# Sliding-window attention and a highway layer in one kernel: the first pair of batches by query blocks, the highway layer on two blocks at a time, the last x transposed by DMA

## The chip, the cores and the metric

The kernel runs on one core of a Trainium2 chip. That core has five engines with instruction queues of their own: PE (TensorE: matrix products and transposes, with results in PSUM), DVE (VectorE), ACT (ScalarE), POOL (GpSimd) and SP (SyncE, which here issues stores). Each engine runs its queue in order and waits on semaphores of the others. The metric is the device time of one execution in microseconds (us).

## The reference

Eight batches, eight heads, 576 positions, head dimension 64. Attention looks back over 128 positions, with a linear bias per head; its output x (4608 rows of 512) goes through a highway layer.

```python
scores = scale * np.matmul(q, k.transpose(0, 1, 3, 2))
rel = pos[:, None] - pos[None, :]
bias = slopes[:, None, None] * (-np.abs(rel))[None, :, :]
mask = (rel >= 0) & (rel < 128)
scores = np.where(mask, scores + bias[None], -1e9)
attn = softmax(scores)                       # max, exp, sum, divide
x = np.matmul(attn, v).transpose(0, 2, 1, 3).reshape(B * S, H * D)
H_ = np.maximum(x @ w_h, 0.0)
T_ = 1.0 / (1.0 + np.exp(-(x @ w_t + b_t)))
out = T_ * H_ + (1.0 - T_) * x
```

Inputs and output are float32; inside the kernel most tiles are bf16, and POOL's loads convert on the way.

## The kernel before, in words

**Duos and stages.** Batches are handled in four duos (m = 0 to 3) of two batches (r = 0, 1). A sequence of 576 positions is four blocks of 128 and a tail block of 64. Duos 1 to 3 have two attention stages each, A (key blocks 0 and 1) and B (key blocks 2, 3 and the tail, 4); duo 0 has four smaller ones, a to d, one for each key block (d also has the tail).

**Loads.** POOL issues the loads that convert. Q and K of a duo come with four neighbouring positions in one partition (L113: 1 KB runs in memory, 512 bytes in SBUF), V and the tails with one position in a partition (L125, L118: 256 bytes in memory, 128 in SBUF). For duo 0, Q and K are cut in two halves of 256 positions, the first half also in two groups of heads. The weight wT comes through POOL (L234), the bias row through L232. The weight wH comes through SP as float32 into the buffer that later takes Q of duo 1 (L222) and is converted by ACT (L228).

**Attention.** PE transposes Q and K (L271; tails L257); DVE or ACT copies the result from PSUM to the tiles `qt` and `kt` (L290, L296, L283). For each head, score products of 64 rows (L329) go to PSUM, the two batches on the two halves of the rows; ACT takes the exponential with the key part of the bias (L345) into `pt`; DVE multiplies by a mask with the rest (L364); PE multiplies with V, which has a column of ones (L393); DVE takes the reciprocal of the sums and writes x (L409, L410).

**Highway layer, block by block (36 blocks of 128 rows).** PE transposes x in four steps (L433), ACT copies it to `xt` (L442), PE makes the product with wH in four matmuls of 512 columns (L449), DVE makes u = max(h, 0) - x (L456), PE makes the product with wT in four (L465) and adds the bias row by a fifth matmul with a one-hot left operand (L467), ACT takes tanh of half of it (L473), POOL (for the last blocks DVE) makes t = 0.5 tanh + 0.5 (L478), DVE multiplies u by t (L483), POOL adds x into the float32 tile `ot` (L489; the very last block DVE), and SP stores it in four parts (L505; the tail blocks in two, L497).

**What sets the order.** All steps are nodes in a dictionary, each with an engine, a planned cost, a priority and dependencies. The order in which they are issued is not computed in the kernel: a list of 762 numbers, `ISSUE`, gives it, and a list `BANKS` gives the PSUM bank (of eight) that each step takes. Since every engine runs in order, these lists set each engine's queue. The SBUF tiles come from small pools: three buffers each of x, `uu`, `tt` and `ot`, five of `xt`. The planned costs serve the search for the order only; they are in the code (`node(..., cost, ...)`), among them 1250 ns on SP and 1000 ns to land for a block of x transposed by DMA, a step (`f_xd`) that the kernel before has and does not use, its list `DMA_X` being empty.

In PE's queue the steps of attention of one duo lie between highway steps of the duo before. After the last product of weights and V there are seven highway blocks left.

Of the kernel before, what the change touches and what calls it, by code (L numbers as in the profile page):

```python
# [14 lines left out]
def kernel(  # L15
# [30 lines left out]
        "a": ((0, 0, 0), (0, 1, 128)),  # L46
        "b": ((1, 1, 0), (1, 2, 128)),
        "c": ((2, 2, 0), (2, 3, 128)),
        "d": ((3, 3, 0), (3, 4, 128), (4, 4, 192)),
    }  # L50
    ORDER = ("abcd", "AB", "AB", "AB")
    DMA_X = ()

    HOME = {"A": ("A", 0), "B": ("B", 0), "a": ("A", 0), "b": ("A", 256), "c": ("B", 0), "d": ("B", 256)}

    GROUPS = {
        "A": ((0,), (1,), (2,), (3,)), "B": ((0,), (1,), (2,), (3,), (4,)),
        "a": ((0,), (1,)), "b": ((0,), (1,)), "c": ((0,), (1,)), "d": ((0,), (1,), (2,)),
    }

    ADD_MASK = ()
# [36 lines left out]
    def load_qk(m, w, x=None, hs=None):  # L98
        src, dst = ((q, QL), (k, KL))[w]
        ps = slice(0, P) if x is None else slice(64 * x, 64 * x + 64)  # L100
        for r in (slice(0, 2),) if hs is None else (0, 1):
            hh = slice(0, H) if hs is None else slice(4 * hs, 4 * hs + 4)
            if hs is None:
                o = dst[m % 2][ps].rearrange("p r h n -> p (r h) n")
                i = src[2 * m : 2 * m + 2, :, 4 * ps.start : 4 * ps.stop, :].rearrange(
                    "r h (p t) d -> p (r h) (t d)", t=4
                )
            else:
                o = dst[m % 2][ps, r, hh, :]
                i = src[2 * m + r, hh, 4 * ps.start : 4 * ps.stop, :].rearrange(  # L110
                    "h (p t) d -> p h (t d)", t=4
                )
            nc.gpsimd.dma_start(out=o, in_=i)  # L113
# [22 lines left out]
    MKA = ADD_MASK and cp.tile([P, H, 2 * P], BF16, name="mka")  # L136
    cvec = cp.tile([P, H], F32, name="cvec")
    ones1 = cp.tile([P, P], BF16, name="ones1")
    wH = cp.tile([P, NCK, DM], BF16, name="wH")
# [25 lines left out]


    BIG = float(2**20)

    def c_mka():
        nc.vector.tensor_scalar(out=MKA[:, :, 0:P], in0=bc(tri[:, 0, :], P), scalar1=BIG,  # L170
                                scalar2=-BIG, op0=ALU.mult, op1=ALU.add)
        for h in range(H):
            nc.vector.tensor_scalar(
                out=MKA[:, h, P : 2 * P], in0=tri[:, 1, :], scalar1=BIG,
                scalar2=-BIG - P * slopes[h] / scale, op0=ALU.mult, op1=ALU.add,
            )

# [13 lines left out]
    def c_vec():  # L191
        nc.vector.memset(ones1[:], 0.0)
        nc.vector.memset(ones1[0:1, :], 1.0)
        nc.vector.memset(bT[:], 0.0)
        for h in range(H):
            nc.vector.memset(cvec[:, h : h + 1], float(np.exp(-float(P) * slopes[h])))
# [20 lines left out]

    def w_stage():
        return QL[1][:].rearrange("p r h n -> p (r h n)").bitcast(F32)

    def load_wf():
        nc.sync.dma_start(  # L222
            out=w_stage().rearrange("p (c n) -> p c n", c=NCK),
            in_=moe_w_h.rearrange("(c p) n -> p c n", p=P),
        )

    def cast_wf():
        nc.scalar.copy(out=wH[:].rearrange("p c n -> p (c n)"), in_=w_stage())  # L228

    def load_w(n):  # L230
        if n == 2:
            nc.gpsimd.dma_start(out=bT[0:1, :], in_=moe_b_t.rearrange("(o n) -> o n", o=1))  # L232
# [10 lines left out]
    def chunks(m):  # L243
        return (0, 1) if ORDER[m][0] == "a" else (None,)

    def tr_parts(m):

        ps = [(x, hs) for x in chunks(m) for hs in range(4 if x is None else 2)]
        return ps + ["tail"]

    def transposes(m, w, part):
# [11 lines left out]
        x, hs = part  # L263
        L = (QL, KL)[w][i]
# [12 lines left out]
    def evac(m, w, part):  # L277
# [7 lines left out]
        x, hs = part  # L285
        nh, n0, n = (2, 0, P) if x is None else (4, 64 * x, 64)
# [14 lines left out]
    def width(kind):  # L301
        return 512 if kind in "AB" else 256

    def scores(m, kind, h):
        i, W = m % 2, width(kind)
        if W == 512 or h % 2 == 0:
            SC[m, kind, h] = ps_tile(2)
        else:
            SC[m, kind, h] = SC[m, kind, h - 1]
        sc, o = SC[m, kind, h], 0 if W == 512 else (h % 2) * W  # L310
        qm = QT[i][:, h, 0:512].rearrange("p (t c q) -> p c t q", t=4, c=4)
        segs, n, add = STAGES[kind], 0, m == 0 and kind in ADD_MASK
        if add and h % 2 == 0:
            for r in range(2):
                nc.tensor.matmul(
                    out=sc[:, r, :], lhsT=ident[:],
                    rhs=MKA[:, h : h + 2, :].rearrange("p h n -> p (h n)"),
                    start=True, stop=False,
                )
        while n < len(segs):  # L320
            j, qb, off = segs[n]
            two = n + 1 < len(segs) and segs[n + 1][0] == j and segs[n + 1][1] < 4
            for r in range(2):
# [3 lines left out]
                else:  # L327
# [4 lines left out]
                    rhs=rhs, start=not add,  # L332
                    stop=not add or (h % 2 == 1 and n + 1 + two >= len(segs)),
# [3 lines left out]
    def soft(m, kind, h):  # L337
        W, (home, c0) = width(kind), HOME[kind]
        if h % 2 == 0:
            if c0 == 0:  # L340
                PT[m, home, h // 2] = ptp[home].tile([P, 2, 2, 512], BF16, name="pt")
            for j, qb, off in STAGES[kind]:
                COL[m, h // 2, j, qb] = (PT[m, home, h // 2], c0 + off)
        o = 0 if W == 512 else (h % 2) * W
# [447 lines left out]
```

The softmax here doesn't subtract the row's maximum and nothing guards it: scores larger than these inputs give would overflow.

## Time and profile before

| what | value |
|---|---|
| time, median of 11 runs | 174.98 us (174.52 to 176.22) |
| profiled execution: its own time | 176.02 us |
| profiled execution: span of the instructions | 174.3 us |
| PE busy | 149.2 us (86%), 2109 matmuls |
| DVE / ACT / POOL busy | 139.9 / 125.2 / 118.6 us |
| loads by POOL's queue | 14.68 MB as written to SBUF, 62832 packets |
| transfers by SP's queue (stores, wH) | 10.49 MB, 7312 packets |

The profile is of one execution. Spans count from its first instruction. A busy time is the time in which an engine ran an instruction; a row of a group gives line, engine, operation, output and inputs, count, and then busy time, the mean of one in ns, and the idle time before them with what ended it. The chain of waits is the work that ended last, followed back through what released each step; the lines of it give start, length and what ran. In the stretches, the columns are: from and to, length, then the busy time of PE, of PE's weight loads, of DVE, ACT and POOL, each with the number of instructions, then the clock granted to PE, the share of the DMA engines and GB/s moved.

### The profile page before, as it was taken

To read this page: it belongs to the slowest core of one execution; us is meant where nothing else is said; L and a number is where in the kernel's file an instruction comes from. 1 tells how busy PE (TensorE), PEld (TensorE's weight loads), DVE (VectorE), ACT (ScalarE), POOL (GpSimd) and SP (SyncE) were. 2 spreads that over 40 slices of the span, in tenths; PEclk is the share of its full clock that TensorE was granted. 3 is DMA by queue.
4 is the path that set the end of the run, shared out by engine and by line. 5 is a ranking of instruction groups with operands and counts; after the bars stand their busy time and mean duration, and the time that the engine had idled before them with its cause. 6 is when DMAs were issued, how large, how long until landed. Compare 5 with 4: busy or idle time off the path is not lost.

```text
span 174.3 us, 5232 instructions
## 1 busy us (share of the span) xinstructions
PE 149.2 (86%) x2109; PEld 92.9 (53%) x2132; DVE 139.9 (80%) x244; ACT 125.2 (72%) x178; POOL 118.6 (68%) x132
## 2 busy tenths in 40 slices
PE   0169688999989979999999979999999999999930
PEld 0158444576646537767556655566556556754410
DVE  5087596889998978999877999889887889986570
ACT  2625568597988988899679968799898887235510
POOL 7897284189893799994058886783485969676540
PEclk9999999999999999999999999999999999999996
DMA  4999999999999999999999997493224232445543
GB/s 147 225 193 190 153 197 183 180 177 114 183 197 212 194 110 152 224 216 213 250 108 163 116 183 103 76 140 101 50 66 120 64 94 72 107 113 122 129 121 90
DMA packets 70167, 25.50 MB, mean 146 GB/s; under 512 B 48128, under 2 KB 65024, under 8 KB 70144
## 3 DMA queue, kind: packets, MB, share of 16 engines
q0 software_dynamic: 62832, 14.68, 120.0%
q1 hardware_dynamic: 7312, 10.49, 22.5%
q8 instruction: 16, 0.26, 0.7%
q14 instruction: 7, 0.06, 0.1%
HBM read 30.41 MB, written 9.44 MB: 229 GB/s over the span
## 4 chain that ended last, share of the span: by engine, by line
PE 50%; DMA 19%; DVE 15%; issue 6%; POOL 4%; ACT 3%; SPq 0%; POOLq 0%; DVEq 0%; ACTq 0%
PE ps L449 13%; PE ps L465 13%; DMA va<-in_v_dram 8%; PE ps L329 7%; PE ps L393 6%; DMA ql<-in_q_dram 6%; PE ps L433 4%; DVE pt L364 4%; DMA kl<-in_k_dram 3%; PE ps L467 3%; PE ps L271 3%; DVE x L410 3%; DVE qt L290 2%; ACT pt L345 2%; DVE uu L483 2%
## 5 line engine op out<-in xcount | busy, mean ns | idle before, releaser
L345 ACT ACTIVATE pt<-ps,bias 128x1024 bf16<-128x1024 f32 (+1 forms) x80 | 72.2, 948 | 14.0 <-PE ps L329 13.8
L489 POOL TENSOR_TENSOR ot<-uu,x 128x512 f32<-128x512 bf16 x35 | 47.6, 1364 | 25.3 <-DVE uu L483 25.3
L364 DVE TENSOR_TENSOR pt<-pt,mk 128x2048 bf16<-128x2048 bf16 (+1 forms) x40 | 45.6, 1153 | 0.8 <-ACT pt L345 0.8
L449 PE MATMUL ps<-wH,xt 128*128 128x512 bf16 x129 | 35.8, 393 | 2.6 <-DVE qt L290 1.0
L465 PE MATMUL ps<-wT,xt 128*128 128x512 bf16 x136 | 36.3, 380 | 1.4 <-DVE uu L456 0.8
L473 ACT ACTIVATE tt<-ps 128x512 f16<-128x512 f32 x36 | 21.6, 604 | 13.0 <-PE ps L467 11.9
L456 DVE SCALAR_TENSOR_TENSOR uu<-ps,x 128x512 bf16<-128x512 f32 x36 | 24.5, 683 | 5.0 <-PE ps L449 4.7
L478 POOL TENSOR_SCALAR tt<-tt 128x512 f16<-128x512 f16 x32 | 22.3, 704 | 8.8 <-ACT tt L473 8.5
L329 PE MATMUL ps<-qt,kt 64*128 64x256 bf16 (+2 forms) x384 | 24.9, 249 | 3.6 <-DVE qt L290 1.1
L410 DVE TENSOR_TENSOR x<-ps,rd 128x256 bf16<-128x256 f32 (+3 forms) x40 | 25.5, 638 | 1.4
L125 POOL DMA_DIRECT2D va<-in_v_dram x20 | 22.3, 1114 | 5.8 <-DMA ql<-in_q_dram 4.1
L393 PEld LDWEIGHTS <-pt 128*128 128x128 bf16 (+1 forms) x576 | 21.0, 101 | 7.6 <-issue 2.5
L393 PE MATMUL ps<-va,pt 128*128 128x65 bf16 (+1 forms) x576 | 24.6, 198 | 0.0
L442 ACT COPY xt<-ps 128x512 bf16<-128x512 bf16 x36 | 20.7, 590 | 5.3 <-PE ps L433 4.1
L483 DVE TENSOR_TENSOR uu<-uu,tt 128x512 bf16<-128x512 bf16 x36 | 19.7, 555 | 3.6 <-POOL tt L478 3.4
L449 PEld LDWEIGHTS <-xt 128*128 128x128 bf16 x144 | 13.1, 100 | 16.0 <-issue 3.5
L329 PEld LDWEIGHTS <-kt 64*128 64x128 bf16 x384 | 13.3, 96 | 13.1 <-issue 9.1
L465 PEld LDWEIGHTS <-xt 128*128 128x128 bf16 x144 | 12.9, 97 | 13.6 <-issue 1.5
L271 PE MATMUL ps<-ident,kl 128*64 128x128 bf16 (+1 forms) x320 | 12.1, 228 | 8.2 <-DMA kl<-in_k_dram 7.9
L296 ACT COPY kt<-ps 128x1024 bf16<-128x1024 bf16 x13 | 13.1, 1016 | 5.6 <-PE ps L271 5.6
L271 PEld LDWEIGHTS <-kl 128*64 128x64 bf16 (+1 forms) x320 | 9.9, 126 | 10.0 <-DMA kl<-in_k_dram 8.5
L290 DVE COPY qt<-ps 128x1024 bf16<-128x1024 bf16 x16 | 11.0, 685 | 4.2 <-PE ps L271 4.2
(44 smaller groups left out, 125.5 us busy)
## 6 DMA issues: line engine op xcount, KB each, us to landing
out_dram<-ot SPq DMA_DIRECT2D x128, 64.0 KB, 2.7
va<-in_v_dram POOLq DMA_DIRECT2D x16, 256.0 KB, 13.6
ql<-in_q_dram POOLq DMA_DIRECT2D x3, 1024.0 KB, 15.1
kl<-in_k_dram POOLq DMA_DIRECT2D x3, 1024.0 KB, 15.2
ql<-in_moe_w_h_dram SPq DMA_DIRECT2D x1, 1024.0 KB, 5.4
out_dram<-ot SPq DMA_DIRECT2D x8, 128.0 KB, 2.4
kl<-in_k_dram POOLq DMA_DIRECT2D x4, 128.0 KB, 5.6
ql<-in_q_dram POOLq DMA_DIRECT2D x4, 128.0 KB, 5.9
```

What stands on the lines that cost most here:

```text
L125: nc.gpsimd.dma_start(out=VA[m % 2][0:n, c, :, :, 0:D].rearrange("s r h d -> s (r h) d"), in_=v[2 * m : 2 * m + 2, :, c * P : c * P + n, : ...
L271: nc.tensor.transpose(out=pt[r * D : (r + 1) * D, c : c + n], in_=L[ps, r, nh * hs + hl, t * D : (t + 1) * D], identity=ident[ps, ps],)
L329: nc.tensor.matmul(out=sc[:, r, o + off : o + off + w_], lhsT=KT[i][rows, h, j * P : (j + 1) * P], rhs=rhs, start=not add, stop=not add or ...
L345: nc.scalar.activation(out=PT[m, home, h // 2][:, h % 2, :, c0 : c0 + W], in_=SC[m, kind, h][:, :, o : o + W], func=ACTF.Exp, bias=BIAS[:, ...
L364: nc.vector.tensor_tensor(out=o, in0=o, in1=mk.to_broadcast([P, 2, rep, W]), op=ALU.mult,)
L393: nc.tensor.matmul(out=av[rows, hl, n * (D + 1) : (n + 1) * (D + 1)], lhsT=pt[:, hl, r, off : off + (D if narrow else P)], rhs=va[:, j, r, ...
L410: nc.vector.tensor_tensor(out=x.rearrange("p b (h d) -> p h b d", h=2), in0=av[:, :, :, 0:D], in1=rd[:, :, 0:nb].to_broadcast([P, 2, nb, D ...
L449: nc.tensor.matmul(out=AH[m, kind, gi], lhsT=XT[m, kind, gi][:, i, c, :], rhs=wH[:, c, :], start=c == 0, stop=c == NCK - 1)
L456: nc.vector.scalar_tensor_tensor(out=uu[:, 0:n, :], in0=AH[m, kind, gi].rearrange("p (i n) -> p i n", i=1), scalar=0.0, in1=x, op0=ALU.max ...
L465: nc.tensor.matmul(out=az, lhsT=XT[m, kind, gi][:, i, c, :], rhs=wT[:, c, :], start=c == 0, stop=False)
L483: nc.vector.tensor_tensor(out=uu, in0=uu, in1=TT.pop((m, kind, gi))[:, 0:n, :], op=ALU.mult)
L489: eng.tensor_tensor(out=ot[:, 0:n, :], in0=UU.pop((m, kind, gi))[:, 0:n, :], in1=x, op=ALU.add)
```

## The change

- **Duo 0 by query blocks.** Stages e, f, g, h have the scores that finish query block 0, 1, 2 and 3 with the tail. Q and K of blocks 0 and 1 come one position in a partition (`load_nat`, into the buffer that later takes K of duo 1), block 0 in two groups of heads; blocks 2 and 3 as before, in one piece.
- **wH through POOL.** The load through SP and the conversion on ACT are gone; wH is now loaded as wT is. In POOL's queue it is the 19th transfer, after K and Q of duo 0, its tails and V blocks 0 and 1. POOL's queue starts with K of blocks 2 and 3, then Q of block 0 (half of the heads), Q of blocks 2 and 3, and the other parts of block 0 and block 1.
- **Highway layer in pairs.** The blocks are taken two at a time (16 pairs; the four tail blocks stay single): one ACT copy, one u, one tanh, one t, one product with t for both, with two PSUM banks each for the products. The sum into `ot` stays one instruction per block. The bias of a pair is now put in first, by two matmuls of 64 rows (`f_zb`), from a second one-hot tile `hot2` and two copies of the bias row.
- **x of the last duo by DMA.** `DMA_X = (8, 9)`: for stages A and B of duo 3, `xt` is made by nine transposing DMAs on SP in place of PE transposes and ACT copies.
- **A new order.** `ISSUE` (670 numbers) and `BANKS` are new. PE's queue starts with the transposes of Q of block 0, then K and Q of blocks 2 and 3, and the scores of e follow the last transposes of block 0. After the last product of weights and V, ten highway blocks are left: the pairs of duo 3's A and B, and two tail blocks, the last steps being gate of duo 2's tail, then duo 3's tail. SP's queue has the nine transposes among the stores: both pairs of A, the second pair of B, a store, the first pair of B, three stores, the tail, and the last stores. On POOL, t and the two sums of a pair stand in a row; its last steps are t of the last pair, t of duo 2's tail, the pair's two sums and the tail's sum.
- Some planned costs are new, and unused code (an additive mask) is gone.

```diff
-        "a": ((0, 0, 0), (0, 1, 128)),
-        "b": ((1, 1, 0), (1, 2, 128)),
-        "c": ((2, 2, 0), (2, 3, 128)),
-        "d": ((3, 3, 0), (3, 4, 128), (4, 4, 192)),
+        "e": ((0, 0, 0),),
+        "f": ((1, 1, 0), (0, 1, 128)),
+        "g": ((2, 2, 0), (1, 2, 128)),
+        "h": ((2, 3, 0), (3, 3, 128), (3, 4, 256), (4, 4, 320)),
     }
-    ORDER = ("abcd", "AB", "AB", "AB")
-    DMA_X = ()
+    ORDER = ("efgh", "AB", "AB", "AB")
+    DMA_X = (8, 9)
...
-        "A": ((0,), (1,), (2,), (3,)), "B": ((0,), (1,), (2,), (3,), (4,)),
-        "a": ((0,), (1,)), "b": ((0,), (1,)), "c": ((0,), (1,)), "d": ((0,), (1,), (2,)),
+        "A": ((0, 1), (2, 3)), "B": ((0, 1), (2, 3), (4,)),
+        "e": ((0, 1),), "f": ((0, 1),), "g": ((0, 1),), "h": ((0, 1), (2,)),
...
+    def load_nat(w, b, hs):
+        src = (q, k)[w]
+        if hs is None:
+            nc.gpsimd.dma_start(
+                out=nat(w, b).rearrange("p r h d -> p (r h) d"),
+                in_=src[0:2, :, b * P : (b + 1) * P, :].rearrange("r h s d -> s (r h) d"),
+            )
+            return
+        for r in range(2):
+            hh = slice(4 * hs, 4 * hs + 4)
+            nc.gpsimd.dma_start(
+                out=nat(w, b)[:, r, hh, :],
+                in_=src[r, hh, b * P : (b + 1) * P, :].rearrange("h s d -> s h d"),
+            )
...
-    def load_wf():
-        nc.sync.dma_start(
-            out=w_stage().rearrange("p (c n) -> p c n", c=NCK),
-            in_=moe_w_h.rearrange("(c p) n -> p c n", p=P),
-        )
-
-    def cast_wf():
-        nc.scalar.copy(out=wH[:].rearrange("p c n -> p (c n)"), in_=w_stage())
...
+        if x in ("n0", "n1"):
+            hh = heads(part)
+            for h in hh:
+                for r in range(2):
+                    c = (h - hh.start) * P
+                    nc.tensor.transpose(
+                        out=pt[r * D : (r + 1) * D, c : c + P],
+                        in_=nat(w, int(x[1]))[:, r, h, :], identity=ident[:],
+                    )
+            return
...
     def f_h(m, kind, gi, i):
-        AH[m, kind, gi] = ps_tile(1)
+        n = grp(m, kind, gi)[1]
+        if i == 0:
+            AH[m, kind, gi] = ps_tile(n).rearrange("p (i n) -> p i n", i=1) if n == 1 else ps_tile(n)
         for c in range(NCK):
-            nc.tensor.matmul(out=AH[m, kind, gi], lhsT=XT[m, kind, gi][:, i, c, :],
+            nc.tensor.matmul(out=AH[m, kind, gi][:, i, :], lhsT=XT[m, kind, gi][:, i, c, :],
                              rhs=wH[:, c, :], start=c == 0, stop=c == NCK - 1)
...
+    def f_zb(m, kind, gi):
+        AZ[m, kind, gi] = ps_tile(2)
+        for i in range(2):
+            rows = slice(i * D, (i + 1) * D)
+            nc.tensor.matmul(out=AZ[m, kind, gi][:, i, :], lhsT=hot2[rows, :], rhs=bT[rows, :],
+                             start=True, stop=False)
...
-    def f_out(m, kind, gi, eng):
+    def f_out(m, kind, gi, i, eng):
         bs, n, x = grp(m, kind, gi)
-        ot = op.tile([P, 2, DM], F32, name="ot")
-        OT[m, kind, gi] = ot
-        eng.tensor_tensor(out=ot[:, 0:n, :], in0=UU.pop((m, kind, gi))[:, 0:n, :], in1=x, op=ALU.add)
+        if i == 0:
+            OT[m, kind, gi] = op.tile([P, 2, DM], F32, name="ot")
+        eng.tensor_tensor(out=OT[m, kind, gi][:, i, :], in0=UU[m, kind, gi][:, i, :],
+                          in1=x[:, i, :], op=ALU.add)
```

The step that makes `xt` by DMA is in both kernels and reads:

```python
for i in range(n):
    nc.sync.dma_start_transpose(out=xt[:, i], in_=x[:, i, :])
```

## The prediction

> **What bounds the kernel now.** I read the stretches first (busy time of each engine between two times), cut where the work changes its kind: the first highway matmul starts at 28.4 us, the last product of weights and V ends at 152.1, the last matmul at 167.1, the span at 174.3.
>
> ```profile
> 28.40:152.10 123.70, 118.06 (x1705) 74.28 (x1725) 109.62 (x178) 103.83 (x140) 86.83 (x87) 1.00 1.59 143
> 152.10:167.10 15.00, 14.77 (x81) 7.06 (x82) 10.43 (x20) 6.29 (x11) 9.85 (x11) 1.00 0.46 115
> 167.10:174.30 7.20, 0.00 (x0) 0.00 (x0) 2.14 (x4) 0.60 (x1) 1.11 (x1) 0.78 0.44 109
> ```
>
> Columns: stretch, length, busy us of PE, its weight loads, DVE, ACT and POOL, granted clock, DMA share, GB/s. From 28.4 to 167.1 us PE is busy 132.8 of 138.7 us at full clock (96%), so PE work taken out there comes off the end nearly one for one; only 5.9 us are gaps. DVE (89% of the long stretch) is the next limit. Before 28.4 and after 167.1 PE doesn't set the time.
>
> Second, the chain of waits, for what a PE step costs in the dense part:
>
> ```profile
> 106.48 0.86 PE ps L465 x4
> 107.34 0.22 PE ps L467
> ...
> 108.64 0.33 PE ps L329 x8
> ...
> 111.43 0.22 PE ps L433 x4
> ```
>
> A gate of one block is 0.86 us, its bias matmul 0.22, the four transposes of x 0.22 (0.33 elsewhere in the chain). Eight score matmuls of 256 columns take 0.33 us; at the gate's rate (0.86 us for 4 x 512 columns) they would take 0.86 one after another, so two matmuls of 64 rows, one on each half of the array, overlap.
>
> Third, the start. The chain runs through transfers until 19.5 us:
>
> ```profile
> 2.14 6.02 DMA kl<-in_k_dram
> 8.44 10.98 DMA ql<-in_q_dram
> ...
> 28.38 3.05 PE ps L449 x7
> ```
>
> ```profile
> 5.00:15.00 10.00, 5.49 (x138) 4.30 (x140) 4.65 (x7) 4.23 (x10) 9.49 (x16) 1.00 1.41 196
> 113.50:116.00 2.50, 2.50 (x48) 1.83 (x49) 1.96 (x4) 2.43 (x4) 2.30 (x2) 1.00 1.91 122
> ```
>
> Last column: 196 GB/s while Q and K come in rows of four positions (512 bytes in SBUF), 122 while only V rows (128 bytes) flow. And POOL's issues wait for old transfers:
>
> ```profile
> POOL va L125 <- DMA ql<-in_q_dram: 4.1, 1, 4.1
> POOL qtl L118 <- DMA ql<-in_q_dram: 3.1, 1, 3.1
> ```
>
> Counting issues, transfer n of POOL's queue starts only when transfer n-8 has landed; so the stream is first come, first served, and its bytes set the start.
>
> **The change, part by part** (minus is gain).
>
> 1. Bias. Removed: 36 x 0.22 = 7.9 us. Added: 4 single blocks x 0.22, and 16 pairs with two 64-row matmuls into two banks. If they overlap like the score pairs, 0.22 a pair, together 4.4, so -3.5; if not, 0.44 a pair and -0.0. I take -3.5: the score rows are the same kind of instruction. A pair's bias now stands ahead of its gates and takes two banks early: the gates queue behind a tanh that still reads them. The plan gives these banks; I charge nothing, and the cover is the 0.86-us gates of other groups.
>
> 2. x of the last duo by DMA. Removed: nine blocks x 0.22 to 0.33 on PE = 2.0 to 3.0, I take -2.4, and nine ACT copies (590 ns, 5.3 us; ACT is 84% busy, so nothing on the path). Added: nine transposing DMAs on SP, of which the trace shows none. Lower bound 0.42 us of SP each (the store's issue, L505); upper 2.7, if each went only when the one before had landed (a 64 KB store takes that long). The planner's table in the code, whose other entries agree with the rows (exp 1118 against 1118 ns), has 1.25 a block and 1 us to land; I take this. Then the last duo's first pair, asked for when its last norm ends, some 6 us before PE reaches it, takes 2.5 + 2. Hidden; +0, the upper bound is a rival. Queued behind on SP: the second pair of B waits for the duo's last norm, and three stores stand behind; their `ot` buffer is wanted again three groups later, some 8 us, against 2.5 us of transposes and 4 issues of 0.42. Covered.
> [...]
>
> 3. Pairs elsewhere. PE: two products with wH back to back save one seam (0.91 against 0.86 us in the chain): 16 x 0.05 = -0.8. ACT: 36 copies of 590 and 36 tanh of 604 ns become 12 of 1016 (L296, 128x1024) and 3 of 590, and 16 of 1118 and 4 of 604: 42.9 to 36.2 us. DVE: u 36 x 683 to 16 x 1220 (L296 on DVE) + 4 x 683, g 36 x 555 to 16 x 730 (L364, 128x1024) + 4 x 555: 44.6 to 36.2. POOL: t 704 ns each, a pair between 704 and 1408, I take 1100; `ot` sums stay one per block. All this lies beside PE: zero on the path, unless the 5.9 us of gaps shrink (a rival).
>
> 4. Start. The stream up to what the first product needs: before, wT is last: 2048 KB of Q and K at 196 GB/s (10.7), V and tails 640 KB at 122 (5.4), wT 512 KB at 196 (2.7) = 18.8 us; it landed at 26.3 (issue 14.40 + 11.9), so an offset of 7.5. After, wH comes through POOL's queue, behind 1024 KB in 512-byte rows (5.4), 1024 KB natural Q and K, 256 KB tails and 512 KB V, all in 128-byte rows (15.0), itself 2.7: 7.5 + 23.1 = 30.6. So the first product starts at about 30.8 and not 28.4: +2.4. Bounds: natural rows at the 145 GB/s seen from 18.5 to 21 us give +0.0; two of its waits for landings not covered (3.1 and 0.8 us) give +6. Against it, more is done by then. Adding the chain's step costs over the order of both kernels, the left-over PE work at that point is 125.8 us before and 118.7 after; 6.0 of the difference is counted in 1 and 2, 1.1 is new. At 1.11 (below) that is 1.2; net +1.2. The ACT cast of wH (1.9 us) goes, beside idle time.
> [...]
>
> 5. Behind the start the stream still leads: wT, tails, K of duo 1 (1024 KB, 5.4) land at 39.8, V block 2 at 41.9, Q of duo 1 at 47.3. PE, at 1.11 us per us of step costs (the dense part's own ratio: 138.7 for 125.8), reaches their users at 39.4, 42.1 and 46.0. +1.3; bounds 0 and 4. POOL's t and `ot` wait behind the blocked issues, three buffers deep: no charge.
>
> 6. Tail. Before, 15 us of PE follow the last weights-V product and 7.2 us the last matmul: 22.2. After, ten blocks (18.8 us) are left, and POOL runs t, g, two sums in a row per pair: 1.1 + 0.7 (DVE) + 2 x 1.15 = 4.1 us against 3.65 of PE. Following both by hand, POOL's last sum (block 4 of duo 2) ends 22.2 us after that product, three pairs of stores on SP (1.7 + 1.1 + 1.1) and 3.1 from last issue to end of the span follow: 28.0, which is 9.2 behind the last matmul: +2.0. Bounds: 0 (order covers POOL) and +4 (sums at 2.1 us, as some in the trace when the mask runs).
>
> Sum: -3.5 - 2.4 - 0.8 + 1.2 + 1.3 + 2.0 = -2.2 us on the profiled execution, 176.02 us long with a span of 174.3 (1.7 around it). It stands 0.6% above the median 174.98; I carry the difference over: 172.8.
>
> **Rivals.**
> A. The gaps close: DVE and ACT each lose 7 to 14 us, and the PE waits on DVE and ACT in the dense part go, 4 of 5.9 us; tail covered. For it: the waits on `qt`, `uu` and `pt` are the named ones. Against: each is 1 us or less, spread. 172.8 - 4 - 2 = 166.8.
> B, the other side. Transposing DMAs are not pipelined (2.7 us each). The last single block's x has nine of them and four stores (6.8) ahead on SP: -6 + 24.3 + 6.8 + 2 = 27 us after the last weights-V product, then 2 us of PE and 7.2 of tail: 36.3 against 28.0. 172.8 + 8.3 = 181.1. It decides from 2.0 us a block (12 + 9 x 2.0 = 30, the forecast's 28.0 and the 2.2 us gained).
> C. The stream is later still (first product at 34, duo 1's Q at 51): 3 + 2 more, 177.8. For it: small packets and POOL's waits; against: no other traffic on it.
> D. The bias pair doesn't overlap: 3.5 back, 176.3.
>
> **How the numbers follow.** About 0.3% (0.5 us) is what can be told from no change. Forecast 0.44 (own range 170 to 175.5: in it 0.35 faster, 0.05 same, 0.04 slower), A 0.23, B 0.11, C 0.16, D 0.06. Faster 0.58, same 0.05, slower 0.37. The range takes in D, C and all of A but its lower end: 166.5 to 178.5; left out are B and some 0.09 of A.
>
> **What would show it.** Right: matmuls of the bias in pairs that start together; no x transposes on PE after the last duo's scores; first wH matmul at 30 to 32 us, waiting for the wH transfer; PE over 95% busy from then to the last matmul; end 9 us behind it, last on POOL. Wrong: `xt` waits on SP's transposes, PE gaps before `kl` and `va` users beyond 50 us, or POOL far behind from the first duo on.

## The result: 1.1% slower, and the profile after

The changed kernel takes 177.1 us (median of 12 runs, 176.22 to 178.24), the kernel before 175.09 us beside it (47 runs). The ratio is 1.0109, interval 1.0084 to 1.0134. The forecast was 172.8 us, range 166.5 to 178.5: the time lies in the range, on the wrong side of no change. Ratios leave out single executions that were disturbed and ran longer, medians do not, and the profiles of the first shift, of the shift alone and of the early DMA are of such executions.

The profiled execution has an own time of 177.07 us and a span of 175.4. Its stretches, cut at the first highway matmul, at 152 us as before, at the last matmul and at the end of the span (the last product of weights and V now ends earlier, at 145.3, with ten blocks left):

```profile
28.85:152.00 123.15, 115.04 (x1669) 71.29 (x1688) 99.79 (x151) 98.56 (x106) 77.79 (x72) 0.99 1.44 146
152.00:166.79 14.79, 13.29 (x64) 5.45 (x62) 8.76 (x11) 4.25 (x5) 10.62 (x10) 1.00 0.78 193
166.79:175.40 8.61, 0.00 (x0) 0.00 (x0) 2.63 (x3) 0.60 (x1) 2.33 (x3) 0.64 0.50 122
```

The start costs 0.45 us (28.85 against 28.40), the dense part is 0.76 shorter (137.94 against 138.7), the tail 1.41 longer (8.61 against 7.2): together +1.1, the difference of the spans. The profile of before is of an execution 0.9 us above its median (176.02 against 175.09 us), that of the changed kernel is at its median; so these 1.1 us are about half of the 2.0 us between the medians, and the rest is in neither profile. The dense part is what did not deliver. In it PE is busy 128.33 us (115.04 + 13.29) where it was busy 132.8, so 4.5 us of work are gone, but its gaps have grown from 5.9 to 9.6 us. The waits of PE between 28 and 167 us name them:

```profile
PE ps L285 <- issue: 2.3, 1, 2.3
PE ps L466 <- DMA xt<-x: 1.4, 1, 1.4
PE ps L447 <- DVE x L421: 1.1, 2, 0.6
```

(Engine and line, what it waited for, total, times, longest.) The first is strange: L285 is a transpose of Q and K, and it waited for nothing that the profile shows. The chain of waits has the place:

```profile
43.44 0.64 PE ps L285 x16
44.08 0.55 PE ps L447 x8
44.63 1.89 PE ps L285 x58
46.52 2.30 issue
48.83 0.36 PE ps L285 x6
```

Groups of 32, 16 and 16 transposes run without a break. Of the last sixteen PE does ten, stops for 2.3 us, and then does the other six, which read the same tile. In all seven profiles that have the stop it lies behind the same 58 transposes. What follows, in stretches of a microsecond (the third figure from the end is the granted clock):

```profile
49.00:50.00 1.00, 1.00 (x30) 0.85 (x26) 0.69 (x1) 0.44 (x1) 0.00 (x0) 0.90 1.44 197
50.00:51.00 1.00, 0.78 (x8) 0.29 (x4) 0.66 (x2) 1.00 (x2) 0.00 (x0) 0.50 1.69 185
51.00:52.00 1.00, 1.00 (x4) 0.16 (x4) 0.63 (x2) 0.06 (x1) 0.29 (x1) 0.50 2.35 161
52.00:53.00 1.00, 1.00 (x7) 0.32 (x7) 0.00 (x0) 0.36 (x1) 1.00 (x2) 0.50 2.44 156
53.00:54.00 1.00, 1.00 (x6) 0.29 (x6) 0.08 (x1) 0.75 (x1) 1.00 (x2) 0.89 2.35 169
```

PE runs at half clock for some 3.4 us, which makes its work about 1.7 us longer (an estimate: half of 3.4; two matmuls of L466 in a row start 0.43 us apart at 51 us, and 0.22 at 53.3 us, behind it). In the profile before, the clock was 1.00 throughout the dense part. The ledger is then: PE work without the half clock 132.8 to 126.6, -6.2; half clock +1.7; gaps +3.7, which are the stop (2.3) and the wait for `xt` (1.4). Sum -0.8.

The other lines that answer to those shown of before: the chain's prices, and the start.

```profile
106.78 0.97 PE ps L466 x4
...
109.13 0.39 PE ps L483 x2
109.52 0.32 PE ps L492
```

```profile
wH<-in_moe_w_h_dram POOLq DMA_DIRECT2D x1, 512.0 KB, 8.9
```

```profile
10.00:13.00 3.00, 2.41 (x70) 2.07 (x67) 1.59 (x3) 0.30 (x4) 3.00 (x4) 1.00 2.26 153
13.00:16.00 3.00, 1.82 (x24) 1.29 (x24) 2.55 (x5) 0.66 (x2) 3.00 (x5) 1.00 2.02 129
16.00:19.00 3.00, 2.66 (x59) 2.23 (x60) 1.73 (x3) 2.59 (x7) 3.00 (x6) 1.00 2.41 153
```

The bias of a pair (L483) takes 0.39 us in the chain here, not the 0.22 that the forecast took. The natural rows of Q and K came at 129 to 153 GB/s (last column), not at 122; wH, issued at 17.76 us, landed 8.9 us later at 26.7, and no matmul waited for it.

### The profile page after: what moved, and what is told of

Same layout as the page of the kernel before. It is cut to its first block, busy times and chain, and to the rows that moved or that the text cites. A ratio compares the mean times of both kernels' runs of the same rounds, so it can differ in the third digit from the quotient of the medians.

```text
span 175.4 us, 4937 instructions
## 1 busy us (share of the span) xinstructions
PE 146.4 (83%) x2059; PEld 91.6 (52%) x2080; DVE 128.2 (73%) x213; ACT 117.6 (67%) x142; POOL 115.0 (66%) x122
## 4 chain that ended last, share of the span: by engine, by line
PE 64%; DVE 15%; DMA 6%; issue 5%; ACT 5%; POOL 1%; DVEq 0%; ACTq 0%; POOLq 0%
PE ps L466 17%; PE ps L492 17%; PE ps L404 9%; PE ps L343 7%; PE ps L285 6%; DVE x L421 5%; DMA ql<-in_q_dram 4%; ACT pt L358 3%; DVE pt L375 3%; PE ps L447 3%; DVE uu L473 2%; PE ps L483 2%; PE ps L273 2%; DMA xt<-x 2%; DVE rd L420 1%
## 5 line engine op out<-in xcount | busy, mean ns | idle before, releaser
L358 ACT ACTIVATE pt<-ps,bias 128x1024 bf16<-128x1024 f32 (+3 forms) x80 | 71.7, 947 | 14.9 <-PE ps L343 14.7
L517 POOL TENSOR_TENSOR ot<-uu,x 128x512 f32<-128x512 bf16 x35 | 42.3, 1224 | 17.7 <-DVE uu L511 17.0
L375 DVE TENSOR_TENSOR pt<-pt,mk 128x2048 bf16<-128x2048 bf16 (+3 forms) x40 | 40.5, 1029 | 4.1 <-ACT pt L358 4.0
L466 PE MATMUL ps<-wH,xt 128*128 128x512 bf16 x133 | 35.6, 390 | 3.5 <-DMA xt<-x 1.4
L506 POOL TENSOR_SCALAR tt<-tt 128x1024 f16<-128x1024 f16 (+1 forms) x18 | 19.0, 1061 | 27.1 <-ACT tt L501 27.1
L501 ACT ACTIVATE tt<-ps 128x1024 f16<-128x1024 f32 (+1 forms) x20 | 18.8, 940 | 19.7 <-PE ps L492 15.2
L343 PE MATMUL ps<-qt,kt 64*128 64x128 bf16 (+2 forms) x432 | 25.6, 243 | 2.6 <-ACT qt L305 0.9
L473 DVE SCALAR_TENSOR_TENSOR uu<-ps,x 128x1024 bf16<-128x1024 f32 (+1 forms) x20 | 22.2, 1112 | 6.9 <-PE ps L466 6.2
L466 PEld LDWEIGHTS <-xt 128*128 128x128 bf16 x144 | 13.3, 100 | 18.6 <-issue 3.6
L511 DVE TENSOR_TENSOR uu<-uu,tt 128x1024 bf16<-128x1024 bf16 (+1 forms) x20 | 14.4, 723 | 5.7 <-POOL tt L506 5.5
L457 ACT COPY xt<-ps 128x1024 bf16<-128x1024 bf16 (+1 forms) x15 | 13.9, 930 | 4.9 <-PE ps L447 4.9
L420 DVE RECIPROCAL rd<-ps 128x4 f32<-128x4 f32 (+3 forms) x40 | 7.9, 198 | 7.6 <-PE ps L404 7.5
```

Of the source, the lines that this page charges most:

```text
L343: nc.tensor.matmul(out=sc[:, r, o + off : o + off + w_], lhsT=KT[i][rows, h, j * P : (j + 1) * P], rhs=rhs, start=True, stop=True,)
L358: nc.scalar.activation(out=PT[m, home, no, h // 2][:, h % 2, :, c0 : c0 + W], in_=SC[m, kind, h][:, :, o : o + W], func=ACTF.Exp, bias=BIA ...
L375: nc.vector.tensor_tensor(out=o, in0=o, in1=mk.to_broadcast([P, 2, rep, W]), op=ALU.mult,)
L466: nc.tensor.matmul(out=AH[m, kind, gi][:, i, :], lhsT=XT[m, kind, gi][:, i, c, :], rhs=wH[:, c, :], start=c == 0, stop=c == NCK - 1)
L473: nc.vector.scalar_tensor_tensor(out=uu[:, 0:n, :], in0=AH[m, kind, gi], scalar=0.0, in1=x, op0=ALU.max, op1=ALU.subtract,)
L501: nc.scalar.activation(out=tt[:, 0:n, :], in_=AZ[m, kind, gi], func=ACTF.Tanh, scale=0.5)
```

## The experiments

The page of the changed kernel lists a DMA queue for instructions with 16 packets and 0.26 MB, 16 KB each. PE's 4139 records of matmuls and weight loads make about 259 for each of the 16, and from the first packet to the last PE ran 250 of them a packet, which is why I take the queue to be the one that fetches PE's program.

```profile
q8 instruction: 16, 0.26, 0.6%
```

From the packets of this queue, beside PE's records (worked out from the traces; start and length in microseconds; the stop is PE's longest idle time in this stretch):

```
kernel                      fetches between 38 and 56    stop of PE
before                      43.53 (2.00), 50.97 (1.06)   1.0 (a wait for qt)
changed                     46.27 (1.13), 53.20 (1.25)   2.3
changed, shifted (below)    41.01 (1.36), 48.19 (0.95)   none
```

In the changed kernel the fetch starts about 3 us later than the distances in the shifted one let expect (an estimate). Counted in PE's own records it is late too: when this fetch starts, PE has run 1207 of them, 1175 to 1209 in the seven profiles with the stop, against 1011 to 1088 in the seven without. PE runs dry 0.25 us after the fetch has started, and goes on 1.4 us after it is done (1.3 to 1.7 us in the seven). The fetch starts as a burst of small packets ends: from 42 to 45 us the loads' packets, nearly all of 128 bytes, take some 90 to 115 ns in the mean, where such packets take 32 to 33 at 51 to 53 us.
**Theory F**: the late fetch makes the stop, and the stop the half clock; together about 4 us. **Rival D**: data or a PSUM bank that the profile does not show. **Beside them** the terms of the forecast, each to be measured by itself.

### The changed kernel again

> The changed kernel as it is, beside the kernel before on the same chip: 1.1% slower (about 177.0 us), with the hole of 2.3 us in PE's queue at 46.5 us and the granted clock at half from 49.8 to 53.2 us.

177.29 us, ratio 1.0136 (1.0091 to 1.018). The stop is there (at 46.0 us, 2.3 us long), the half clock too. The wait for `xt` is not: the last wH product waits 0.7 us for a tanh instead, whose bank it takes. So the stop came again, in a second execution, and the `xt` wait did not.

### The program shifted, first attempt

Sixty spare transposes of 128x128 into a bank that is empty then, behind the identity, at the head of PE's queue; nothing reads their result:

```diff
+            if key == ("ident",):
+                for _ in range(60):
+                    nc.tensor.transpose(out=PSB[:, 7, :].bitcast(BF16)[:, 0:P], in_=ident[:], identity=ident[:])
```

> The changed kernel with 60 spare transposes of the identity into an unused PSUM bank at the start of PE's queue, where PE waits for its first load anyway; they compute nothing that is used. They shift PE's program by 120 instructions against the 16 KB pieces in which it is fetched. Theory F (the hole at 46.5 us is PE's program arriving late, because its fetch stood behind a burst of slow 128-byte packets, and the half clock follows from the idle time): the fetch is asked for before the burst at 41.5 us, hole and half clock are gone there, and the time falls by 3 to 4 us, to 173 to 174. Rival D (PE waits there for a load or a bank): the hole stays where it is and the time stays within 1 us of the changed kernel.

177.33 us, 1.009 (1.0053 to 1.0127). The stop at 46 us is gone (the fetch came at 42.98), but half clock now lay between 17 and 30 us. A gain at one place and a new loss at another: the run does not decide.

### The program shifted without the early load

Forty spare transposes of 64x64, where PE waits 1.2 us anyway; with their weight loads they make 80 records:

```diff
+            if key == ("s", 0, "e", 0):
+                for _ in range(40):
+                    nc.tensor.transpose(out=PSB[0:D, 7, :].bitcast(BF16)[:, 0:D], in_=ident[0:D, 0:D], identity=ident[0:D, 0:D])
```

> Only addition: 40 spare transposes of 64x64 into the bank that stands empty, emitted behind the first score group, where TensorE waits for 1.2 us anyway. [...] If the late program fetch makes the hole (theory F): no hole of 2.3 us near 46 us, no half clock at 50 to 53 us, and 177.2 - 2.3 - 1.7 = 173.2 us (172.3 to 174.5). If data or a bank made the hole (theory D): the hole stays at the same transposes and the time is 177 us. If the hole only moves to another fetch: 175 to 177 us with a hole of 1 us or more somewhere else at a fetch.

The stop and the half clock are gone. The stretch that held both, 46 to 54 us, in this run and in the changed kernel:

```profile
46.00:54.00 8.00, 7.95 (x110) 4.29 (x105) 6.92 (x11) 7.28 (x9) 7.07 (x7) 1.00 1.86 182
```

```profile
46.00:54.00 8.00, 5.48 (x57) 2.38 (x55) 2.99 (x6) 3.98 (x5) 4.42 (x5) 0.79 1.85 183
```

PE works 7.95 us of 8 at full clock where it worked 5.48 at 0.79; the runs below that have the same shift and an addition show the same 7.95 at 1.00. Rival D falls: loads and banks of the kernel's own steps are as they were. But the time is 1.0077 (1.0031 to 1.0122), 177.98 us in the median of 12, and not 0.99. Where did 4 us go? The clearest view is one that I worked out from PE's records: the time at which PE starts the same step, less that of the changed kernel.

```
step at, in   changed  POOL order  shift   shift and  shift and
the changed   again    alone       alone   tail       POOL order
   43.3       -0.52    -0.06       +0.13    +0.85      +0.73
   54.4       -0.54    -0.41       -3.90    -3.18      -3.30
   81.6       -0.54    -0.41       -3.90    -2.19      -3.30
   86.1       -0.54    -0.41                -1.02      -3.29
   93.0       -0.54    -0.41                -0.06      -2.91
  112.2       -0.54    -0.41                -0.05      -2.91
  160.0       -0.54    -0.40                -0.04      -2.90
  165.3       -1.22    -1.72                -1.62      -4.21
```

(The column of the shift alone is read up to 82 us only.) The shift takes 4.0 us out between 43 and 54 us, the size expected. Then, in the run with shift and tail, something between 70 and 95 us takes it back, and behind that it runs in step with the changed kernel to 160 us. There is a second limit, that PE does not reach while the stop holds it up.

### Shift and tail

The shift, with the tail's edits told further down:

> The shift by 40 small transposes and the tail together. If the two losses are separate: 177.2 - 4.0 - 2.0 = 171.2 us (170.5 to 173.0), under the 175.0 of before. If the hole only moves: 173 to 175.5.

1.0027 (0.9993 to 1.0061), 176.70 us: over both expected ranges. The stop is gone again, and the lead falls from 3.2 to 0.06 us. POOL's timeline there:

```profile
79.08 0.68 POOL L134 DMA_DIRECT2D qtl<-in_q_dram  x1 [5.97 <-DMA kl<-in_k_dram]
79.79 0.63 POOL L506 TENSOR_SCALAR tt<-tt 128x512 f16<-128x512 f16 x1
81.47 0.71 POOL L134 DMA_DIRECT2D ktl<-in_k_dram  x1 [1.05 <-DMA va<-in_v_dram]
83.81 0.68 POOL L134 DMA_DIRECT2D ktl<-in_k_dram  x1 [1.63 <-DMA va<-in_v_dram]
86.38 0.81 POOL L141 DMA_DIRECT2D va<-in_v_dram  x1 [1.90 <-DMA va<-in_v_dram]
87.21 3.67 POOL L517 TENSOR_TENSOR ot<-uu,x 128x512 f32<-128x512 bf16 x2
```

and PE's waits from 76 to 100 us:

```profile
PE ps L285 <- DVE qt L314: 1.1, 1, 1.1
PE ps L343 <- DVE uu L473: 0.7, 1, 0.7
```

POOL stands 6 us in front of a load of duo 3's tails, and again in front of the next three, each time until an older transfer has landed (as the prediction counted out; in the changed kernel's trace each of the 50 loads from the ninth on starts 0.28 us or more after transfer n-8 has landed, and 12 of them before n-7 has; in the trace of before it is 46 loads, with the same 0.28 us). The tails are not wanted for more than 20 us: their transposes start at 105 and 112 us. Behind the loads in POOL's queue stand a gate (L506) and the sums (L517) that DVE waits for; DVE then evacuates late, and PE waits for its banks. The loads do not land earlier when PE is earlier: K of duo 3 was issued at 57.8 us here and at 61.0 in the changed kernel, and landed at 78.8 here and at 75.6 there. So POOL, which comes to the next issues earlier, stands longer; in the changed kernel it issued the same loads with one wait of 1.6 us.

### Shift and POOL's order

The shift, and the three loads behind the work that stood after them. In this run and the next the last two banks of the list are also 3 and 4 in place of 2 and 0, an edit of the tail told further down; it touches only the last block of the highway layer.

```diff
 POOL: ... qk.3.0
-      tl.3.0  t.0h1  tl.3.1  v.3.4  o.0h0.0  o.0h0.1  t.1A1  o.0h1.0
+      t.0h1  o.0h0.0  o.0h0.1  tl.3.0  tl.3.1  t.1A1  o.0h1.0  v.3.4
       o.1A1.0  o.1A1.1  v.2.2 ...
```

> The shift by 40 small transposes, and on POOL three loads of duo 3 (both tails, V block 4) moved behind the sums and gates of duo 0 and 1 that stood after them; nothing else moves. In the run with the shift alone TensorE was 3.9 us ahead of the changed kernel up to 82 us, and lost 6.1 us between 82 and 98 us; there POOL stood 5.3, 0.8, 1.5 and 2.1 us in front of these loads (each issue waits for an older transfer to land), the gates and sums behind them came late, and VectorE and a bank of scores waited for them. If the blocked POOL takes the lead (theory P): TensorE passes 98 us with the lead kept, and the end is 3 to 4 us under the changed kernel's, 0.988 to 0.993 of the kernel before (173.0 to 174.3 us). If VectorE's masks, which took 5.5 to 6.0 us there instead of 1.2, are slow by themselves and not through what POOL does beside them (theory V): most of the lead is still lost, 1.003 to 1.012.

174.16 us, 0.9931 (0.9896 to 0.9966): faster than both kernels, by 0.7% under the kernel before. Against the changed kernel's 1.0109 that is 0.982, or 3.1 us. The lead is kept (3.30 at 81.6, 2.91 from 93 to 160 us), and POOL no longer waits for a load:

```profile
POOL tt L506 <- DMA out_dram<-ot: 4.7, 1, 4.7
POOL ot L517 <- DVE uu L511: 3.8, 1, 3.8
POOL tt L506 <- ACT tt L501: 1.3, 2, 0.7
```

(POOL's waits from 70 to 90 us; none of the three is for a load, the first being for a store, and PE's longest wait from 54 to 100 us is 0.5 us.) The two masks of DVE at 84 us take 2.36 us together, so they are not slow by themselves (theory V). The stretches, cut at the first highway matmul's weights, the last matmul and the end:

```profile
29.85:162.55 132.70, 126.58 (x1732) 76.37 (x1750) 107.71 (x160) 102.90 (x111) 86.92 (x81) 1.00 1.41 156
162.55:172.60 10.05, 0.00 (x0) 0.00 (x0) 4.34 (x6) 0.60 (x1) 3.71 (x3) 0.68 0.43 105
```

The dense part is 132.7 us, 6.0 under the 138.7 of before, with 126.6 us of PE work and 6.1 of gaps. It starts 1.0 us later than in the changed kernel; half clock lay ahead of it here, from 26.2 to 29.6 us.

### POOL's order alone

> The POOL order alone, without the shift: the hole at 46 us and the half clock stay, so TensorE comes late enough for POOL's blocked issues to hurt little. Theory P: within 0.5 us of the changed kernel, 1.008 to 1.014 of before. If the POOL order gains by itself (gates and sums earlier everywhere): 1.000 to 1.006.

176.80 us, 1.0056 (1.002 to 1.0091), inside the range that was given for a gain of the order by itself. The trace puts the gain elsewhere. Up to 160 us this run is 0.4 ahead of the changed kernel, and that lead arose at the stop (1.9 us here), not where POOL's order differs: up to there the order alone does nothing. The rest came at 162 us, where PE had no wait for `xt` or a bank; this run had the two other banks too, so that part can't be put down to the order.

From the changed kernel's 1.0109 the shift alone takes 0.3% (1.0077) and this run 0.5%, neither clear of the changed kernel's interval; both together take 1.8%. The banks are the same in two other runs that differ in POOL's order and in one more output buffer: shift and tail (1.0027) and the last of the tail runs below (0.9937), 0.9% apart. Together with the table, which shows the lead kept with the new order and lost without it, this says that the gain of the shift reaches the end only with POOL's order.

### The spare transposes in the kernel before

> The kernel before, with the same 40 spare transposes of 64x64 into its empty bank 7, where TensorE waits 1.1 us for ScalarE (12 us). In its profile no program fetch came late (the longest stop of TensorE between 28 and 167 us is 1.2 us). If the spare transposes help only through the one late fetch of the changed kernel (theory F): no gain here, 0.997 to 1.003. If they help by themselves, by a warmer clock or an order that settles better: 0.98 to 0.99, as in the changed kernel. If the new position meets a burst of loads and makes a fetch late in this kernel too: a hole of 2 us or more with half clock behind it, 1.01 to 1.025.

174.94 us, 0.9992 (0.9963 to 1.0022), clock 0.992. No gain and no loss: the spare work does nothing by itself in a kernel without the stop. (Its own fetch that meets the burst, at 39.98, took 2.27 us and held nothing up.)

### The bias of a pair by full-height matmuls

Two matmuls of 128 rows at the end of the gates, as before the change, in place of the two of 64 rows ahead:

```diff
-        for i in range(2):
-            rows = slice(i * D, (i + 1) * D)
-            nc.tensor.matmul(out=AZ[m, kind, gi][:, i, :], lhsT=hot2[rows, :], rhs=bT[rows, :], start=True, stop=False)
...
-                             start=one and c == 0, stop=not one and c == NCK - 1)
-        if one:
+                             start=c == 0, stop=False)
+        if True:
```

> The changed kernel with the bias of a pair added as before, by one full-height matmul at the end of each gate, in place of the two half-height ones ahead of them. If the two halves overlap and cost 0.22 us a pair, this adds 16 x 0.22 = 3.5 us of PE work; if the half-height pair costs 0.3 to 0.4 us with the change of shape, as its lines in the chain say, it adds 0.6 to 2 us.

179.28 us, 1.0243 (1.0208 to 1.0278): 1.9 to 2.3 us over the changed kernel (against 1.0136 on the same chip, and 1.0109). The edit is worth 2 us, not 3.5. Removed were 32 x 0.22 = 7.0, so a pair costs (7.0 - 2.0) / 16 = 0.31 us. The two matmuls do overlap (109.130 and 109.136 us start, 0.37 and 0.39 long); but as a pair they stand 0.26 to 0.39 us in the chain, where a full-height one in a row of its kind costs 0.22.

### x of the last duo by TensorE again

Only this part undone, with the five groups of transposes and copies put by hand between the steps of the last 30 us:

```diff
-    DMA_X = (8, 9)
+    DMA_X = ()
```

> The changed kernel with the last duo's x transposed by TensorE and copied by ScalarE again (the transposes placed by hand, one bank each), all else as it is. By the prediction's own term for the DMA the time goes up by 2.4 us to 179.6; if the wait for xt at 161.8 us (1.4 to 1.8 us of TensorE) took back most of the gain it rises by 0.6 to 1.0 us to 178; if the DMA was worth nothing or less it is 177.2 or below.

179.97 us, 1.0211 (1.0161 to 1.0261): 1.3 to 1.8 us over the changed kernel. The DMA is worth most of the 2.4 us. In the profile this run starts the step at 160 us 2.2 us after the changed kernel, though it had been 0.3 ahead at 138; between the two, where the transposes are, it loses 2.5. (Its stop was 1.5 us long, and no half clock followed it.)

### The tail, three ways

First, the last block's transposing DMA moved on SP, nothing else:

```diff
 SP: ... x.3B0
+    x.3B2
     st.2B1  st.3A0  st.3A1
-    x.3B2
     st.3B1 ...
```

> The changed kernel with one step moved in SP's queue: the transposing DMA of duo 3's tail block is issued right behind the first pair of B, ahead of three groups of stores. If the wait of 2.8 us for xt at 161.8 us sets the end, PE ends 1.8 us sooner and the time falls by 1 to 2 us; if POOL's last sums set the end, as the prediction's tail had it, it falls by under 0.5 us.

178.25 us, 1.0157 (1.0105 to 1.021): no gain. The last wH product waited not for `xt` but for ACT, whose tanh held its bank 2, as in the second execution of the changed kernel:

```profile
166.35 1.02 ACT tt L501
...
167.44 0.61 ACT tt L501
...
168.09 1.02 PE ps L466 x4
```

Second, the same with banks that were free (3 and 4 for 2 and 0), and three of POOL's last operations on DVE (the gate and the sum of duo 2's tail, the second sum of the last pair):

```diff
-                e, cost = ("DVE", (350, 600)) if last and gi else ("POOL", (640, 1070))
+                e, cost = ("DVE", (350, 600)) if last and gi or kb == (2, "B", 2) else ("POOL", (640, 1070))
...
-                e, cost = ("DVE", 640) if end else ("POOL", 1160)
                 for i in range(n):
+                    e, cost = ("DVE", 640) if end or (kb, i) in (((2, "B", 2), 0), ((3, "B", 0), 1)) else ("POOL", 1160)
```

> Tail only: the last block's transposing DMA goes right behind the pair's before it, its wH product takes a bank that was free long before (3 for 2; in the earlier run with the early DMA it waited for ScalarE to free bank 2 instead of for xt), and three of POOL's last operations go to VectorE: the t of the last block of duo 2, its sum, and the second sum of the last pair. Everything up to 155 us, the hole at 46 included, stays. If the tail is limited by the wait for xt and by POOL's last sums: TensorE ends 1.4 us earlier, the end follows 8.0 in place of 8.6 us after it, 177.2 - 2.0 = 175.2 us (174.5 to 176.0). If VectorE becomes the tail's limit, or the store queue: 176.5 to 177.5.

177.85 us, 1.0099 (1.0063 to 1.0136): no gain that can be told from the changed kernel. PE ends 1 us earlier (its last matmul started at 165.4, not 166.4), and the span ends 0.2 us later. The chain ran through a store:

```profile
160.70 2.27 POOL ot L517 x2
...
162.99 0.32 SPq L534
...
163.35 2.27 DMA out_dram<-ot
...
165.66 0.42 DVE uu L511
```

A sum waited until the store before it had read its output buffer. Third, a fourth output buffer, together with the shift and POOL's order:

```diff
-        "pA": 5, "pB": 4, "x": 3, "xt": 5, "uu": 3, "tt": 3, "ot": 3,
+        "pA": 5, "pB": 4, "x": 3, "xt": 5, "uu": 3, "tt": 3, "ot": 4,
```

> The same, with the tail of the tail run and one more output buffer (4 for 3): in the tail run the last sums moved to VectorE waited 1.3 us for an output buffer that a store still held. If the tail's limit was that buffer: 1.0 to 1.6 us less than the run with the shift and the POOL order alone, 0.980 to 0.987 of before. If the order of stores on SP is the limit: the same as that run within 0.4 us.

174.81 us, 0.9937 (0.9901 to 0.9973), the same as without the tail's edits (which but for the banks are all that is added). SP still issues the last eight stores one after another, 0.3 to 0.6 us each, from 165.9 to 170.1 us. Three waits were seen at the end (`xt` or a bank, a buffer, the stores); taking away the first two gained nothing. That the stores are the last of them fits the expectation, and was not tested by moving them.

## Why the prediction was wrong

**The step that failed** is the one on which the sum rests: PE at 96% with full clock, "so PE work taken out there comes off the end nearly one for one". The work came out (132.8 to 126.6, -6.2), and its place was taken by 4.0 us of stop and half clock; with the stop gone, POOL's blocked issues took 3 us back; only with both limits gone is the dense part 6.0 us shorter. The forecast had -6.6 us for this part (-3.5 - 2.4 - 0.8 - 1.2 + 1.3), and -0.8 came: the 5.8 us between are, within 0.2, stop and half clock (4.0), the bias (1.5) and the wait for `xt` (1.4), less the 1.3 of item 5 that did not come. That the total was off by less is luck: the start was 1.95 and the tail 0.6 us better than forecast.

Two things in the views of before were left out of the forecast. The rivals had PE waiting for data, and none had PE waiting for its own program, though the page of before has the line for that queue (16 packets there too) and its packets show a fetch of 2.00 us at 43.53, inside a burst of loads. That this was near could be seen; that the new order would put a fetch where PE runs dry could not. And the chain of before, from which the forecast takes its prices, is not PE's from 38 to 64 us:

```profile
39.51 1.22 POOL ot L489
...
40.99 13.97 DMA va<-in_v_dram
...
55.25 0.68 POOL qtl L118
...
57.56 2.29 POOL va L125 x2
...
62.09 0.59 DVE uu L483
...
63.38 0.69 DVE uu L456
64.12 1.02 PE ps L465 x4
```

The landing of a V load, POOL's issues behind it, and the gates and sums behind those set the time at which PE goes on at 64 us (it waited 0.8 us there). A busy share of 96% says that PE has little slack there, not that it is what the end waits for; a limit of the kind that the shift laid bare stood in this chain.

**Item 1, bias (-3.5)**: -2.0. The two matmuls overlap as forecast, the size is off: a pair is 0.31 us and not 0.22. The row taken was that of score products, of which eight follow one another; a bias pair stands alone between matmuls of full height. That this is what makes it dearer was not tested. The chosen value was an end of the bounds.

**Item 2, x by DMA (-2.4)**: -1.3 to -1.8. SP's issue is 1.26 us a block in the median (1.20 to 2.10), as the planner's table had it, and the landing 2.5 us:

```profile
xt<-x SPq DMA_TRANSPOSE x9, 2.5
```

Rival B (2.7 us each) is excluded. The landing is about that of a store of the same kernel (2.4 us), the issue three times a store's (0.43 us in the median of L534). "Hidden" failed at one block: the tail's DMA stands behind stores, and in the profiled execution PE waited 1.4 us for it. In other executions the bank was the wait there, or neither.

**Item 3 (seams)** was not measured alone; with 1, 2 and the 1.1 of item 4 it gives about the -6.2 of PE work if the bias is taken at its size: -2.0 - 2.4 - 0.8 - 1.1 = -6.3. Its sum for ACT is wrong (the terms give 34.3 us, not 36.2), which does not enter the forecast.

**Item 4, start (+2.4 at the first product)**: +0.45. The 122 GB/s row of lone V rows was taken for rows of 128 bytes; they came at 129 to 153. The other bound (145 GB/s, +0.0) was the better one.

**Item 5, the stream behind the start (+1.3)**: PE waited for no load between 30 and 160 us: 0. But the sentence beside it, "POOL's t and `ot` wait behind the blocked issues, three buffers deep: no charge", is a term put at nothing that the runs with shift and POOL's order overturn. It held for the kernel with the stop in it, and not for the kernel that was forecast: without the stop the blocked issues took 3 us back.

**Item 6, tail (+2.0)**: +1.4. Right in sign and about in size, by some luck: the terms listed add to 29.2 us and not to 28.0 (22.2 + 1.7 + 1.1 + 1.1 + 3.1). Last were the stores of the tail on SP behind DVE's sum, with POOL's last sum ending 0.3 us before it began.

Rivals: A (gaps close) did not come, they are 9.6 us, and 6.1 in the fastest version. B and C did not come; of D's 3.5 us 1.5 came. The slower outcome had 0.37 of the chance, for mechanisms of which only D came, by less than half; what came was a loss of 4.0 us with a cause outside the list.

**What stays open**: why the fetch starts late. That it starts as the burst of slow packets ends was seen in every run with the stop, but the burst was not moved by itself, and before's fetch went through a like burst in 2.0 us. Shown is that moving PE's program by 80 records takes the stop away, with data, banks and loads as they were, and that the same 80 records do nothing in a kernel without the stop.

## What to carry to other kernels

When an engine stops in the middle of a run that has all its data, with "issue" as the only reason, look at the packets of the instruction queue at that time, and at the granted clock after it; here a stretch was 4 us too long with no wait of data to blame. Shift the program by some spare instructions, where the engine waits anyway, and see whether the stop goes. On a queue that both issues loads and computes, put loads that are not urgent behind the sums that others wait for: here this cost nothing while PE was late, and it decided as soon as PE got faster. So a change that yields nothing is not refuted until the next wait behind it has been taken away too.

## What the runs showed of the hardware that was not expected

**Half clock after a short stop.** Stops of 1.9 to 2.4 us were followed, 0.1 to 1.4 us after they ended, by about 3.4 us at 0.50 in five of the seven profiles that had the stop (changed, again, POOL order alone, tail, full-height bias), and not in two (2.5 us with the early DMA, 1.5 us with x on TensorE). In each of the 14 profiles the recorded changes of the granted clock lie whole multiples of 3.41 us apart (in the changed kernel's, half clock begins at 49.80, ends at 53.22 and begins again at 169.27 us: 1 and 34 times 3.41). Cut into windows on that grid, from 30 us to the last matmul, the 14 profiles have 538 windows at full clock. Seven of them had 1.9 us or more of idle PE time (1.91 to 3.18), and each was followed by half clock; the other 531 had 1.8 or less, and none was. (Ahead of 30 us a window with 1.5 us idle was followed by it once, in the run with shift and POOL's order.) The 2.5 us of the early DMA fit this: that stop lay across an edge of the grid, with 1.7 us on one side and 0.85 on the other.

**Masks of DVE that took longer beside POOL.** In the profiles of the first shift, the shift alone and the early DMA one mask of DVE took 5.5 to 6.0 us while POOL ran sums and a gate back to back; these are DVE's row and then POOL's of the run with the shift alone, two masks in 7.11 us in place of 2.36:

```profile
84.62 7.11 DVE L375 TENSOR_TENSOR pt<-pt,mk 128x2048 bf16<-128x2048 bf16 x2 [1.21 <-ACT pt L358]
```

```profile
85.11 2.27 POOL L517 TENSOR_TENSOR ot<-uu,x 128x512 f32<-128x512 bf16 x2
87.34 1.04 POOL L506 TENSOR_SCALAR tt<-tt 128x1024 f16<-128x1024 f16 x1
88.36 1.15 POOL L517 TENSOR_TENSOR ot<-uu,x 128x512 f32<-128x512 bf16 x1
```

The first of the two masks ended at 90.6, 1.1 us after POOL's row. In the run with shift and tail both gave way: two sums took 3.67 us for 2.27, and a mask beside them 2.18 for 1.2. In the profile before, the four masks of 128x2048 that no sum or gate of POOL overlapped took 1.21 to 1.22 us, the twenty others 1.21 to 3.14. That POOL's work is what slowed a mask is read from these times alone; no run tests it. No other reading above rests on these masks.
